# A two-stage Fourier kernel: its outer stages as float32 products on quarters of the array

## The chip, the cores and the metric

The kernel runs on one core of one Trainium2 chip. The metric is the time of one execution on the device in microseconds (us); of several executions the median is given. A profiled execution gives a trace: its span runs from the first to the last instruction.

## The reference

A Fourier layer with a soft threshold, followed by a layer that mixes by a two-dimensional Fourier transform and ends in an MLP:

```python
# x: (8, 3136, 256), float32
X = rfft(x, axis=1)
Yr = Xr @ w_r - Xi @ w_i + b_r;  Yi = Xr @ w_i + Xi @ w_r + b_i
Y = soft_threshold(Yr, 0.01) + 1j * soft_threshold(Yi, 0.01)
a = irfft(Y, n=3136, axis=1)
mixed = real(fft(fft(a, axis=1), axis=2))
u = a + mixed
un = (u - mean(u)) / sqrt(var(u) + 1e-6)          # over the last axis
out = u + relu(un @ w_ch1) @ w_ch2                # 256 -> 1024 -> 256
```

## The kernel before

The 3136 positions of a sequence are n1 (64) times n2 (49), and the transform along them is done in two stages of products with tables. Stage one, `p1`, multiplies 64 values of n1 by a 64 x 64 table and stores the result `a` in DRAM. Stage two, `p2_f2`, works along n2. Then come the weights (`p2_w`), the transform along the last axis for the mixing layer (`p2_mix`, which stores `md`), and the way back: `p2_yt` and `p2_g2` along n2, which store `b`, and `p3_norm` along n1. `p3_norm` loads `b` into `bf` and the mixed values into `mt`, multiplies `bf` by the inverse table, adds `mt` to get `ut`, and takes mean and variance; `p3_tr` transposes `ut` on TensorE, `p3_mlp1` and `p3_mlp2` are the MLP.

The 128 partitions hold two times 64 rows of n1: the two halves of a sequence's n2, 24 rows each, side by side. (The 25th row, `NM - 1`, is a single one that two neighbouring sequences share: the joint row.) So the tables `fwd` and `inv` are 128 x 128 with two blocks of 64 x 64 on the diagonal and zeros elsewhere. `p1` and `p3_norm` work in chunks of two n2 rows, 512 columns of 256 each.

Sequence 0 runs in float32 up to the inverse stage, and the forward stage of sequence 1 too (`te.matmul` with `fwd_f`). All else splits each operand into a high and a low part of type float32r and adds three products. ACT makes the high part, POOL (`lo_g`) or DVE (`lo_v`) the low part:

```python
def mm3(o, lh, ll, rh, rl, start=True, stop=True, first=0):
    ops = [(lh, rh), (lh, rl), (ll, rh)]
```

Each stage of each sequence is a generator that yields the time at which it would like to go on (in units of `T` per sequence); a heap hands them out in that order, and a scheduler orders each engine's instructions from there, taking one whose operands are late behind others. The engines then run their lists in order. The MLP works on groups of 4 n2 rows (`groups`; odd sequences have 25 rows, 4 groups of 4 and 3 of 3), and `clock3` gives each group its due time; `NRM` and `TR` say how long ahead of the MLP of a group its norm and its transposes stand. All DMAs go through SyncE's queue in order. `gtile` hands out 4 PSUM banks, shared by all stages but the MLP.

Of the kernel before, what the change touches and what calls it, by code (L numbers as in the profile page):

```python
# [10 lines left out]
F32 = mybir.dt.float32  # L11
# [38 lines left out]
def order_n2():  # L50

    return np.arange(NM * 2).reshape(2, NM).T.reshape(-1)[:N2]
# [8 lines left out]
def tables():  # L61
# [4 lines left out]
    inv = np.zeros((2, 2, U, 2, 32, 2))  # L66
    n1h = rows_n1()
    for s in range(2):
        for u in range(U):
            ph = 2 * np.pi * ((n1 * u) % N1) / N1  # L70
            if u == 0:
                alt = np.where(n1 % 2, -1.0, 1.0)
                fwd[s, :, s, 0, 0] = 1.0
                fwd[s, :, s, 1, 0] = alt
                inv[s, 0, 0, :, :, s] = 1.0
                inv[s, 1, 0, :, :, s] = np.where(n1h % 2, -1.0, 1.0)
            else:
                fwd[s, :, s, 0, u] = np.cos(ph)
                fwd[s, :, s, 1, u] = -np.sin(ph)
                phh = 2 * np.pi * ((n1h * u) % N1) / N1  # L80
                inv[s, 0, u, :, :, s] = 2 * np.cos(phh)
                inv[s, 1, u, :, :, s] = -2 * np.sin(phh)
# [54 lines left out]
def spectral_block(ctx: ExitStack, tc: tile.TileContext, x, w_ri, b_ri, w1, w2,  # L137
# [68 lines left out]
    fwd_f = cp.tile([128, 128], F32, name="fwd_f")  # L206
    fwd_0 = cp.tile([128, 128], F32, name="fwd_0")
# [11 lines left out]
    def load_consts():  # L219
# [14 lines left out]
        yield 1.6 * T  # L234
        for name in ("wr", "ws", "wd"):
            split(name, KF[name])
        split("fwd", fwd_f)

# [5 lines left out]
        inv = sb.tile([128, 128], F32, tag="mt", bufs=2, name="inv_f")  # L244
        nc.sync.dma_start(out=inv, in_=c_inv)
        split("inv", inv)
# [113 lines left out]
    def ask(b, ci, todo, slots, pre):  # L360

        tag, bufs, z, i = slots[ci]
        if i or ci in pre:
            return
        m, n = todo[ci]
        xf = pre[ci] = sb.tile([128, 512 * z], F32, tag=tag, bufs=bufs, name="xf")
        nn = n if n == 1 else 2 * z
        behind(BEHIND if b == 1 else 7, out=xf[:, :nn * D].rearrange("p (n d) -> p n d", d=D), in_=x_rows(b, m, nn))

    def p1(b):  # L370
# [8 lines left out]
        todo = chunks + [(NM - 1, 1)] * (b % 2 == 0)  # L379
        t0, width = T1 if b == 1 else (b - 0.3, 0.75)  # L380
        rooms = [("W2", 1, 4), ("W3", 1, 4)] + [("utl", 2, 2)] * 2 if b == 1 else [("xf", 2, 1)] * len(todo)
        slots = [(tag, bufs, z, i) for tag, bufs, z in rooms for i in range(z)]
        evs = [("bf", 2), ("bf", 2), ("bh", 2), ("bh", 2), ("bl", 2), ("bl", 2), ("ev", 2), ("ev", 2)] * 2
        pre = {}
        if b == 1:
            yield T * ASK
            for ci in range(0, 12, 2):
                ask(b, ci, todo, slots, pre)
        for ci, (m, n) in enumerate(todo):
            yield T * (t0 + width * ci / len(todo))  # L390
            w = n * D
            ask(b, ci, todo, slots, pre)
            tag, bufs, z, i = slots[ci]
            xf = pre[ci - i][:, i * 512:i * 512 + 512]
            g = gtile("g_f1")
            if b == 1:
                te.matmul(g[:, :w], fwd_f, xf[:, :w], start=True, stop=True)
            else:
                xh = sb.tile([128, 512], F32R, tag="xh", bufs=1, name="xh")
                xl = sb.tile([128, 512], F32R, tag="xl", bufs=1, name="xl")  # L400
                sc.copy(xh[:, :w], xf[:, :w])  # L401
                lo_g(xl[:, :w], xf[:, :w], xh[:, :w])
                mm3(g[:, :w], *K["fwd"], xh[:, :w], xl[:, :w])
            tag, bufs = evs[ci] if b == 1 else ("ev", 2)
            ev = sb.tile([128, 512], F32, tag=tag, bufs=bufs, name="ev")
            (va.tensor_copy if ci % 2 and b != 1 else sc.copy)(ev[:, :w], g[:, :w])
            evv = ev[:, :w].rearrange("p (n d) -> p n d", d=D)
            if n == 1:
                for r in range(2):
                    st_eng.dma_start(out=a_dram[b + r](0)[0][m, 0].rearrange("c u d -> (c u) d"), in_=evv[r * 64:r * 64 + 64, 0])  # L410
            else:
                st_eng.dma_start(out=n2_rows(a_dram[b](0)[0], m, n), in_=evv)
# [254 lines left out]
    def p2_g2(b):  # L667

        bd = b_dram[b] = dr.tile([NM, 2, 2, U, D], F32, tag="bd", bufs=4, name=f"bd{b}")
        for q in range(4):  # L670
            base, STEP, F2W, W0, WW, M0 = clock2(b, q)
            for i in range(4):
# [11 lines left out]
                bev = sb.tile([98, 512], F32, tag="bl" if b == 0 and i % 2 else "bev", bufs=2, name="bev")  # L684
# [6 lines left out]
    groups = [[(4 * i, 4) for i in range(6)], [(4 * i, 4) for i in range(4)] + [(16 + 3 * i, 3) for i in range(3)]]  # L691
    parts_of = {z: [(i, min(2, z - i)) for i in range(0, z, 2)] for z in (3, 4)}
# [6 lines left out]
    def p3_norm(b):  # L699

        for gi, (g0, z) in enumerate(groups[b % 2]):
            t0, T3 = clock3(b, g0)
            for i, n in parts_of[z]:
                yield t0 + T3 * (NRM + i / 4)
                yield from after(("b", b), ("m", b))
                m = g0 + i
                w = n * D
                joint = m == NM - 1

                bf = sb.tile([128, 512], F32, tag="bf", bufs=2, name="bf")  # L710
                mt = sb.tile([128, 2, D], F32, tag="mt", bufs=2, name="mt")
                bfv = bf[:, :w].rearrange("p (n d) -> p n d", d=D)
                if joint:
                    for r in range(2):
                        nc.sync.dma_start(out=bfv[64 * r:64 * r + 64, 0], in_=b_dram[b - 1 + r][m, 0].rearrange("c u d -> (c u) d"))
                else:
                    nc.sync.dma_start(out=bfv, in_=n2_rows(b_dram[b], m, n))
                for r in range(2):
                    bb, n2 = (b - 1 + r, m) if joint else (b, NM * r + m)
                    mpn, mmn = (d[0:NH].rearrange("(a n2) d -> a n2 d", n2=N2) for d in m_dram[bb])  # L720
                    if joint:
                        nc.sync.dma_start(out=mt[r:64:2, 0], in_=mpn[:, n2])
                    elif r == 0:
                        nc.sync.dma_start(out=mt[:64, :n], in_=bass.AP(
                            tensor=mpn.tensor, offset=mpn[:, n2].offset, ap=[[N2 * D, 32], [NM * D, 2], [1, n * D]]))
                    nc.sync.dma_start(out=mt[64 + r:128:2, :n][:, ::-1], in_=mmn[:, 49 - n2 - n:49 - n2])
                bh = sb.tile([128, 512], F32R, tag="bh", bufs=2, name="bh")
                bl = sb.tile([128, 512], F32R, tag="bl", bufs=2, name="bl")
                sc.copy(bh[:, :w], bf[:, :w])  # L729
# [4 lines left out]
                va.tensor_add(ut[:, :n], g[:, :w].rearrange("p (n d) -> p n d", d=D), mt[:, :n])  # L734
# [12 lines left out]
                gp.tensor_mul(vv[:, :n], vv[:, :n], rs[:, :n])
                gp.tensor_scalar(vv[:, :n], vv[:, :n], -0.5, 1.5, op0=ALU.mult, op1=ALU.add)
                gp.tensor_mul(rs[:, :n], rs[:, :n], vv[:, :n])
                uts[b, gi, i] = ut, rs  # L750

    def p3_tr(b):
        for gi, (g0, z) in enumerate(groups[b % 2]):
            t0, T3 = clock3(b, g0)
            for i, n in parts_of[z]:
# [5 lines left out]
                ut = uts[b, gi, i][0]  # L761
# [27 lines left out]
    def p3_mlp2(b):  # L789
        for gi, (g0, z) in enumerate(groups[b % 2]):  # L790
# [12 lines left out]
            for (i, n), o in zip(parts_of[z], ops):  # L803
                ut, rs = uts.pop((b, gi, i))
# [93 lines left out]
```

## Time and profile before

| | us |
|---|---|
| median of 3 runs | 1915.78 |
| lowest and highest | 1915.67, 1918.73 |
| profiled execution, its time | 1918.35 |
| profiled execution, its span | 1916.6 |
| TensorE busy (PE) | 1858.5 |
| VectorE, ScalarE, GpSimd busy | 1239.4, 838.5, 654.7 |

PE is TensorE's products, PEld its loads of weights, which run beside the products. A float32 product appears in the trace as two instructions of PE, each with a load of its own. A product's length in the trace contains its way through the array, so the lengths of neighbours overlap; the distance between two starts is what a product takes of the engine's time. The mean granted clock of TensorE was 0.984 of full speed. In the views, L162 is the line of `mm3`'s products; `g_f` is the bank of the forward stage, `g_g` that of the inverse stage (and of `p2_g2`), and `o` and `h` are those of the MLP.

### The profile page before, as it was taken

The numbers are of one execution on the slowest core, as the hardware profiler recorded it, in microseconds if no ns is written. First come the engines' busy times: TensorE is split into PE (matmuls) and PEld (weight loads), VectorE is DVE, ScalarE is ACT, GpSimd is POOL, SyncE is SP. The second block draws the span as 40 slices with busy tenths as digits, with TensorE's granted clock in tenths as the row PEclk, the third lists the DMA queues.
The fourth block names the chain that finished last, engine by engine and source line by source line (L and its number), as shares of the span: only waits on it lengthen the run. The fifth ranks groups of instructions, "written<-read, shape, count | busy, mean of one in ns | idle before, by whom it ended". The sixth has DMA issues, their size and how long they took to land.

```text
span 1916.6 us, 33595 instructions
## 1 busy us (share of the span) xinstructions
PE 1858.5 (97%) x12079; PEld 1698.1 (89%) x12079; DVE 1239.4 (65%) x2718; ACT 838.5 (44%) x1851; POOL 654.7 (34%) x1027
## 2 busy tenths in 40 slices
PE   6887999999999999999999999999999999999999
PEld 3557999999999999989999899998999999988999
DVE  3756767766666766667766666666677676665443
ACT  2455544444444444445444444434444343433222
POOL 0006543442334433244333344434334332322110
PEclk8998999999999999999999999999999999999999
DMA  8666543443435434354333543434443332223110
GB/s 247 217 195 197 156 125 101 138 136 111 135 97 154 133 104 120 99 159 138 110 112 105 151 130 114 118 105 135 139 123 101 106 100 65 76 80 109 59 37 25
DMA packets 153279, 232.93 MB, mean 122 GB/s; under 512 B 18256, under 2 KB 98200, under 8 KB 152856
## 3 DMA queue, kind: packets, MB, share of 16 engines
q1 hardware_dynamic: 153112, 230.78, 40.4%
q8 instruction: 95, 1.56, 0.3%
q14 instruction: 72, 0.59, 0.1%
HBM read 127.95 MB, written 102.76 MB: 120 GB/s over the span
## 4 chain that ended last, share of the span: by engine, by line
PE 86%; DMA 6%; DVE 2%; SPq 2%; ACT 2%; issue 1%; POOL 1%; DVEq 0%; POOLq 0%; ACTq 0%
PE o L162 27%; PE h L162 26%; PE g_w L162 9%; PE g_g L162 7%; PE g_f L465 4%; PE g_f L162 3%; PE g_yt L654 2%; PE g_ut L766 2%; PE g_mix L585 1%; DMA md<-mq 1%; DMA bf<-bd 1%; DMA raw_w<-in_w 1%; DMA mt<-md 1%; PE g_mix L587 1%; DMA af<-aq 1%
## 5 line engine op out<-in xcount | busy, mean ns | idle before, releaser
L786 DVE SCALAR_TENSOR_TENSOR hl<-h,hh 128x512 fp32r<-128x512 f32 (+1 forms) x416 | 272.8, 656 | 344.9 <-ACT hh L785 343.4
L162 PE MATMUL o<-w2h,hl 128*128 128x256 f32 x1568 | 454.6, 290 | 3.4 <-DVE hl L786 3.3
L785 ACT ACTIVATE hh<-h 128x512 fp32r<-128x512 f32 (+1 forms) x416 | 238.4, 573 | 491.3 <-PE h L162 448.3
L162 PE MATMUL o<-w2h,hh 128*128 128x256 f32 x1568 | 444.0, 283 | 0.0
L162 PE MATMUL o<-w2l,hh 128*128 128x256 f32 x1568 | 443.9, 283 | 0.0
L162 PE MATMUL h<-utl,w1h 128*128 128x512 f32 (+1 forms) x832 | 325.0, 391 | 0.0
L162 PE MATMUL h<-uth,w1l 128*128 128x512 f32 (+1 forms) x832 | 317.5, 382 | 0.0
L162 PE MATMUL h<-uth,w1h 128*128 128x512 f32 (+1 forms) x832 | 316.6, 381 | 0.0
L162 PEld LDWEIGHTS o<-w2h,hl 128*128 128x128 f32 x1568 | 298.7, 190 | 10.9 <-DVE hl L786 4.6
L162 PEld LDWEIGHTS o<-w2h,hh 128*128 128x128 f32 x1568 | 299.4, 191 | 6.1
L162 PEld LDWEIGHTS o<-w2l,hh 128*128 128x128 f32 x1568 | 299.3, 191 | 0.0
L155 POOL TENSOR_TENSOR bl<-bf,bh 128x512 fp32r<-128x512 f32 x104 | 128.2, 1234 | 278.6 <-ACT bh L729 268.7
L155 POOL TENSOR_TENSOR xl<-xf,xh 128x512 fp32r<-128x512 f32 (+1 forms) x75 | 100.5, 1340 | 277.7 <-ACT xh L401 277.4
L162 PEld LDWEIGHTS h<-uth,w1l 128*128 128x128 f32 x832 | 156.3, 188 | 24.9
L162 PEld LDWEIGHTS h<-utl,w1h 128*128 128x128 f32 x832 | 157.4, 189 | 15.2
L162 PEld LDWEIGHTS h<-uth,w1h 128*128 128x128 f32 x832 | 156.8, 188 | 14.5
L465 PEld LDWEIGHTS g_f<-tff,af 98*128 98x128 f32 x1024 | 146.8, 202 | 22.8 <-issue 11.3
L465 PE MATMUL g_f<-tff,af 98*128 98x100 f32 x1024 | 152.2, 282 | 11.3 <-DMA af<-aq 9.5
L734 DVE TENSOR_TENSOR ut<-g_g,mt 128x512 f32<-128x512 f32 x104 | 68.4, 657 | 82.4 <-PE g_g L162 55.5
L155 POOL TENSOR_TENSOR Xsl<-xs,Xsh 128x200 fp32r<-128x200 f32 x112 | 73.5, 657 | 134.9 <-ACT Xsh L491 129.5
L528 POOL TENSOR_TENSOR Y<-y,m 128x400 f32<-128x400 f32 x56 | 66.0, 1178 | 105.5 <-DVE m L527 78.0
L155 POOL TENSOR_TENSOR Xl<-xx,Xh 128x400 fp32r<-128x400 f32 x84 | 91.0, 1084 | 30.6 <-ACT Xh L482 30.6
(160 smaller groups left out, 3656.1 us busy)
## 6 DMA issues: line engine op xcount, KB each, us to landing
bd<-bev SPq DMA_DIRECT2D x128, 196.0 KB
bf<-bd SPq DMA_DIRECT2D x92, 256.0 KB
out_dram<-ut SPq DMA_DIRECT2D x92, 256.0 KB
af<-ad SPq DMA_DIRECT2D x56, 392.0 KB
md<-mq SPq DMA_DIRECT2D x112, 192.0 KB
ad<-ev SPq DMA_DIRECT2D x84, 256.0 KB
xf<-in_x SPq DMA_DIRECT2D x76, 256.0 KB
mt<-md SPq DMA_DIRECT2D x192, 64.0 KB
```

What stands on the lines that cost most here:

```text
L155: gp.tensor_sub(out_, full, hi.bitcast(F32))
L162: te.matmul(o, l, r, start=start and i == 0, stop=stop and i == 2)
L465: te.matmul(gf[:, k, :, s], afs[s][:, ui * D + k * 128:ui * D + k * 128 + 128], tfs[s][:, ui].rearrange("p (c j) -> p c j", c=2), start=Tr ...
L528: (va if b == 0 or o == 0 else gp).tensor_sub(y[:, o, :, c, :], y1, m)
L585: te.matmul(o, eh[:, e, ui], cs, start=e == 0, stop=False)
L587: te.matmul(o[:, :n], el[:, e, ui], cs[:, :n], start=False, stop=e == 1)
L654: te.transpose(gt[:100, (v * 2 + o) * 128:(v * 2 + o + 1) * 128], y[:, o, place].rearrange("p c j -> p (c j)"), ident)
L734: va.tensor_add(ut[:, :n], g[:, :w].rearrange("p (n d) -> p n d", d=D), mt[:, :n])
L766: te.transpose(gv[:, k, j * 128:(j + 1) * 128], ut[:, j, k * 128:(k + 1) * 128], ident)
L785: sc.activation(hh[:, :w], h[:, :w], AF.Relu)
L786: va.scalar_tensor_tensor(hl[:, :w], h[:, :w], 0.0, hh[:, :w].bitcast(F32), op0=ALU.max, op1=ALU.subtract)
```

## The change

The two outer stages no longer split their operands. A new helper, `quarters`, takes four n2 rows at a time and multiplies, in float32, each half of 64 partitions by its 64 x 64 block; the first two rows of a half write 64 partitions of a bank, the next two the other 64, and the two halves write two banks. The layouts follow: x is loaded 4 rows at a time in one transfer, `order_n2` and the rows of the tables of stage two are permuted, the inverse stage's rows come out with the half outside and n1 inside, `mt` is loaded for four rows by four transfers of 32 partitions, and `bf` by two ahead of the products. The joint rows are single float32 products on the whole array. In odd sequences the MLP's groups become five of 4, one of 2 and one of 3. Sequence 0's forward stage (`p1_first`) stays as it is.

```diff
+    def quarters(banks, mat, movs):
+        for j in range(2):
+            for i in range(2):
+                rows = slice(64 * i, 64 * i + 64)
+                te.matmul(banks[i][64 * j:64 * j + 64], mat[rows, rows], movs[i][j], start=True, stop=True)
...
     def p1(b):
-        todo = chunks + [(NM - 1, 1)] * (b % 2 == 0)
+        todo = [(m, 4) for m in range(0, NM - 1, 4)] + [(NM - 1, 1)] * (b % 2 == 0)
...
-            g = gtile("g_f1")
-            if b == 1:
-                te.matmul(g[:, :w], fwd_f, xf[:, :w], start=True, stop=True)
-            else:
-                xh = sb.tile([128, 512], F32R, tag="xh", bufs=1, name="xh")
-                xl = sb.tile([128, 512], F32R, tag="xl", bufs=1, name="xl")
-                sc.copy(xh[:, :w], xf[:, :w])
-                lo_g(xl[:, :w], xf[:, :w], xh[:, :w])
-                mm3(g[:, :w], *K["fwd"], xh[:, :w], xl[:, :w])
...
+            banks = [gtile("g_f1") for _ in range(2)]
+            quarters(banks, fwd_f, [[xf[64 * r:64 * r + 64, p * 512:p * 512 + 512] for p in range(2)] for r in range(2)])
+            for r, g in enumerate(banks):
+                tag, bufs = evs[(2 * ci + r) % len(evs)]
+                ev = sb.tile([128, 512], F32, tag=tag, bufs=bufs, name="ev")
+                (va.tensor_copy if r and b != 1 else sc.copy)(ev, g)
+                st_eng.dma_start(out=n2_rows(a_dram[b](0)[0], m + 2 * r, 2), in_=ev.rearrange("p (n d) -> p n d", d=D))
...
-    groups = [[(4 * i, 4) for i in range(6)], [(4 * i, 4) for i in range(4)] + [(16 + 3 * i, 3) for i in range(3)]]
+    groups = [[(4 * i, 4) for i in range(6)], [(4 * i, 4) for i in range(5)] + [(20, 2), (22, 3)]]
...
     def p3_norm(b):
-        for gi, (g0, z) in enumerate(groups[b % 2]):
-            t0, T3 = clock3(b, g0)
-            for i, n in parts_of[z]:
-                yield t0 + T3 * (NRM + i / 4)
...
-                sc.copy(bh[:, :w], bf[:, :w])
-                lo_g(bl[:, :w], bf[:, :w], bh[:, :w])
-                g = gtile("g_g1")
-                mm3(g[:, :w], *K["inv"], bh[:, :w], bl[:, :w])
-                ut = sb.tile([128, 2, D], F32, tag="ut", bufs=UTB, name="ut")
-                va.tensor_add(ut[:, :n], g[:, :w].rearrange("p (n d) -> p n d", d=D), mt[:, :n])
...
+        for m, n in [(4 * i, 4) for i in range(6)] + [(NM - 1, 1)] * (b % 2):
+            t0, T3 = clock3(b, m)
+            yield t0 + T3 * (NRM - 0.5 * (n == 1))
+            yield from after(("b", b), ("m", b))
+            mt = sb.tile([128, 4, D], F32, tag="mt", bufs=2, name="mt")
+            bfs = [sb.tile([128, 512], F32, tag="bf", bufs=4, name="bf") for _ in range(1 + (n > 1))]
+            for r in range(2):
+                if n == 1:
+                    nc.sync.dma_start(out=bfs[0][64 * r:64 * r + 64, :D], in_=b_dram[b - 1 + r][m, 0].rearrange("c u d -> (c u) d"))
                 else:
+                    nc.sync.dma_start(out=bfs[r].rearrange("p (n d) -> p n d", d=D), in_=n2_rows(b_dram[b], m + 2 * r, 2))
+            for r in range(2):
+                bb, n2 = (b - 1 + r, m) if n == 1 else (b, NM * r + m)
+                mpn, mmn = (d[0:NH].rearrange("(a n2) d -> a n2 d", n2=N2) for d in m_dram[bb])
+                p = 64 * r
+                nc.sync.dma_start(out=mt[p:p + 32, :n], in_=mpn[:, n2:n2 + n])
+                nc.sync.dma_start(out=mt[p + 32:p + 64, :n][:, ::-1], in_=mmn[:, 49 - n2 - n:49 - n2])
+            if n == 1:
                 g = gtile("g_g1")
+                te.matmul(g[:, :D], inv_f, bfs[0][:, :D], start=True, stop=True)
+                finish(m, 1, g, mt[:, :1])
+                continue
+            banks = [gtile("g_g1") for _ in range(2)]
+            quarters(banks, inv_f, [[bfs[r][64 * p:64 * p + 64] for r in range(2)] for p in range(2)])
+            for p, g in enumerate(banks):
+                finish(m + 2 * p, 2, g, mt[:, 2 * p:2 * p + 2])
```

`finish` holds what followed before: the sum into `ut`, the statistics, the square root and its correction, for two n2 rows.

More of the change, by code (lines that the diff above doesn't have):

```diff
@@ L50, in order_n2 @@
 def order_n2():
-    return np.arange(NM * 2).reshape(2, NM).T.reshape(-1)[:N2]
+    k = np.arange(NM - 1)
+    first = 4 * (k // 4) + k % 2 + NM * (k // 2 % 2)
+    return np.append(np.stack([first, first + 2], 1).reshape(-1), NM - 1)
 def rows_n1():
@@ L65, in tables @@
     fwd = np.zeros((2, N1, 2, 2, U))
-    inv = np.zeros((2, 2, U, 2, 32, 2))
+    inv = np.zeros((2, 2, U, 2, 2, 32))
     n1h = rows_n1()
@@ L74, in tables @@
                 fwd[s, :, s, 1, 0] = alt
-                inv[s, 0, 0, :, :, s] = 1.0
-                inv[s, 1, 0, :, :, s] = np.where(n1h % 2, -1.0, 1.0)
+                inv[s, 0, 0, s] = 1.0
+                inv[s, 1, 0, s] = np.where(n1h % 2, -1.0, 1.0)
             else:
@@ L80, in tables @@
                 phh = 2 * np.pi * ((n1h * u) % N1) / N1
-                inv[s, 0, u, :, :, s] = 2 * np.cos(phh)
-                inv[s, 1, u, :, :, s] = -2 * np.sin(phh)
+                inv[s, 0, u, s] = 2 * np.cos(phh)
+                inv[s, 1, u, s] = -2 * np.sin(phh)
     tf = np.zeros((2, N2, U, 2, S))
@@ L206, in spectral_block @@
     fwd_f = cp.tile([128, 128], F32, name="fwd_f")
+    inv_f = cp.tile([128, 128], F32, name="inv_f")
     fwd_0 = cp.tile([128, 128], F32, name="fwd_0")
@@ L234, in load_consts @@
         yield 1.6 * T
+        nc.sync.dma_start(out=inv_f, in_=c_inv)
         for name in ("wr", "ws", "wd"):
             split(name, KF[name])
-        split("fwd", fwd_f)
         cs = K["cs"] = cp.tile([128, 2, 2, 128], F32R, name="cs")
@@ L243, in load_consts @@
         sc.copy(cs[:, 0, 1, 0:1], t[:, 0, 128:129])
-        inv = sb.tile([128, 128], F32, tag="mt", bufs=2, name="inv_f")
-        nc.sync.dma_start(out=inv, in_=c_inv)
-        split("inv", inv)
     ident = cp.tile([128, 128], F32, name="ident")
@@ L365, in ask @@
         m, n = todo[ci]
-        xf = pre[ci] = sb.tile([128, 512 * z], F32, tag=tag, bufs=bufs, name="xf")
-        nn = n if n == 1 else 2 * z
+        xf = pre[ci] = sb.tile([128, 1024 * z], F32, tag=tag, bufs=bufs, name="xf")
+        nn = n if n == 1 else 4 * z
         behind(BEHIND if b == 1 else 7, out=xf[:, :nn * D].rearrange("p (n d) -> p n d", d=D), in_=x_rows(b, m, nn))
+    def quarters(banks, mat, movs):
[3 more added lines that the diff above has]
+                te.matmul(banks[i][64 * j:64 * j + 64], mat[rows, rows], movs[i][j], start=True, stop=True)
     def p1(b):
@@ L378, in p1 @@
                 a_dram[i] = lambda u, ad=ad: (ad, u)
-        todo = chunks + [(NM - 1, 1)] * (b % 2 == 0)
+        todo = [(m, 4) for m in range(0, NM - 1, 4)] + [(NM - 1, 1)] * (b % 2 == 0)
         t0, width = T1 if b == 1 else (b - 0.3, 0.75)
-        rooms = [("W2", 1, 4), ("W3", 1, 4)] + [("utl", 2, 2)] * 2 if b == 1 else [("xf", 2, 1)] * len(todo)
+        rooms = [("W2", 1, 2), ("W3", 1, 2)] + [("utl", 2, 1)] * 2 if b == 1 else [("xf", 2, 1)] * len(todo)
         slots = [(tag, bufs, z, i) for tag, bufs, z in rooms for i in range(z)]
-        evs = [("bf", 2), ("bf", 2), ("bh", 2), ("bh", 2), ("bl", 2), ("bl", 2), ("ev", 2), ("ev", 2)] * 2
+        evs = [("bf", 4)] * 4 + [("ev", 2)] * 2 if b == 1 else [("ev", 2)]
         pre = {}
@@ L386, in p1 @@
             yield T * ASK
-            for ci in range(0, 12, 2):
+            for ci in range(len(todo)):
                 ask(b, ci, todo, slots, pre)
@@ L390, in p1 @@
             yield T * (t0 + width * ci / len(todo))
-            w = n * D
             ask(b, ci, todo, slots, pre)
-            tag, bufs, z, i = slots[ci]
-            xf = pre[ci - i][:, i * 512:i * 512 + 512]
-            g = gtile("g_f1")
-            if b == 1:
-                te.matmul(g[:, :w], fwd_f, xf[:, :w], start=True, stop=True)
-            else:
-                xh = sb.tile([128, 512], F32R, tag="xh", bufs=1, name="xh")
-                xl = sb.tile([128, 512], F32R, tag="xl", bufs=1, name="xl")
-                sc.copy(xh[:, :w], xf[:, :w])
-                lo_g(xl[:, :w], xf[:, :w], xh[:, :w])
-                mm3(g[:, :w], *K["fwd"], xh[:, :w], xl[:, :w])
[L404 to L407, printed above, removed]
+            i = slots[ci][3]
+            xf = pre[ci - i][:, i * 1024:i * 1024 + 1024]
             if n == 1:
+                g = gtile("g_f1")
+                te.matmul(g[:, :D], fwd_f, xf[:, :D], start=True, stop=True)
+                ev = sb.tile([128, 512], F32, tag="ev", bufs=2, name="ev")
+                sc.copy(ev[:, :D], g[:, :D])
                 for r in range(2):
-                    st_eng.dma_start(out=a_dram[b + r](0)[0][m, 0].rearrange("c u d -> (c u) d"), in_=evv[r * 64:r * 64 + 64, 0])
-            else:
-                st_eng.dma_start(out=n2_rows(a_dram[b](0)[0], m, n), in_=evv)
+                    st_eng.dma_start(out=a_dram[b + r](0)[0][m, 0].rearrange("c u d -> (c u) d"), in_=ev[r * 64:r * 64 + 64, :D])
+                continue
[6 more added lines that the diff above has]
+                st_eng.dma_start(out=n2_rows(a_dram[b](0)[0], m + 2 * r, 2), in_=ev.rearrange("p (n d) -> p n d", d=D))
         done.add(("a", b))
@@ L683, in p2_g2 @@
                         mm3(g[:98, cols], tih[:, t], til[:, t], yh[:, cols], yl[:, cols], first=1)
-                bev = sb.tile([98, 512], F32, tag="bl" if b == 0 and i % 2 else "bev", bufs=2, name="bev")
+                bev = sb.tile([98, 512], F32, tag="xf" if b == 0 and i % 2 else "bev", bufs=2, name="bev")
                 (va.tensor_copy if b else sc.copy)(bev, g[:98])
@@ L688, in p2_g2 @@
         done.add(("b", b))
-    groups = [[(4 * i, 4) for i in range(6)], [(4 * i, 4) for i in range(4)] + [(16 + 3 * i, 3) for i in range(3)]]
-    parts_of = {z: [(i, min(2, z - i)) for i in range(0, z, 2)] for z in (3, 4)}
+    groups = [[(4 * i, 4) for i in range(6)], [(4 * i, 4) for i in range(5)] + [(20, 2), (22, 3)]]
+    parts_of = {z: [(i, min(2, z - i)) for i in range(0, z, 2)] for z in (2, 3, 4)}
     uts, uthl, hhl = {}, {}, {}
@@ new lines, in finish @@
+        def finish(m, n, g, mt):
+            ut = sb.tile([128, 2, D], F32, tag="ut", bufs=UTB, name="ut")
+            va.tensor_add(ut[:, :n], g[:, :n * D].rearrange("p (n d) -> p n d", d=D), mt)
+            st = sb.tile([128, 2, 6], F32, tag="st", bufs=2, name="st")
+            ag = sb.tile([128, 2, 2], F32, tag="ag", bufs=2, name="ag")
+            rs = sb.tile([128, 2, 1], F32, tag="rs", bufs=8, name="rs")
+            for j in range(n):
+                va.bn_stats(st[:, j], ut[:, j])
+                va.bn_aggr(ag[:, j], st[:, j])
+            vv = sb.tile([128, 2, 1], F32, tag="vv", bufs=2, name="vv")
+            sc.activation(rs[:, :n], ag[:, :n, 1:2], AF.Sqrt, bias=eps_t)
+            gp.tensor_scalar(vv[:, :n], ag[:, :n, 1:2], 1.0, EPS, op0=ALU.mult, op1=ALU.add)
+            va.reciprocal(rs[:, :n], rs[:, :n])
+            gp.tensor_mul(vv[:, :n], vv[:, :n], rs[:, :n])
+            gp.tensor_mul(vv[:, :n], vv[:, :n], rs[:, :n])
+            gp.tensor_scalar(vv[:, :n], vv[:, :n], -0.5, 1.5, op0=ALU.mult, op1=ALU.add)
+            gp.tensor_mul(rs[:, :n], rs[:, :n], vv[:, :n])
+            uts[b, m] = ut, rs
@@ L890 @@
         for r in range(2):
-            v = y[:, h, :, r]
+            v = y[:, r, h]
             for s in range(2):
```

45 lines of the change are left out of this document (5 added, 40 removed).

## The prediction

> **What bounds the kernel now.** I read the page's parts 1, 2 and 4 first: who is busy, at which clock, and which engine carries the chain.
>
> ```profile
> PE 1858.5 (97%) x12079; PEld 1698.1 (89%) x12079; DVE 1239.4 (65%) x2718; ACT 838.5 (44%) x1851; POOL 654.7 (34%) x1027
> ...
> PEclk8998999999999999999999999999999999999999
> ...
> PE 86%; DMA 6%; DVE 2%; SPq 2%; ACT 2%; issue 1%; POOL 1%; DVEq 0%; POOLq 0%; ACTq 0%
> ```
>
> TensorE is busy for 97% of the span, at the full granted clock in almost every slice, and carries 86% of the chain that ended last. No other engine is over 65%. So the time of this kernel is the time that TensorE needs for its list of products, plus the few places where it stands still. The waits of PE, longest first, say how few these are:
>
> ```profile
> PE g_ut L766 <- DVE ut L734: 17.1, 5, 5.7
> PE g_f L465 <- DMA af<-aq: 9.5, 1, 9.5
> PE g_f L338 <- DMA xf<-in_x: 4.4, 3, 3.7
> PE g_g L162 <- ACT bh L729: 3.9, 1, 3.9
> ```
>
> Only the first belongs to the changed stages: the transposes of `p3_tr` wait five times for the sum `ut` of `p3_norm`. Work taken from ACT, DVE or POOL is therefore worth nothing by itself; work taken from TensorE counts almost one to one.
>
> **The terms removed.** The groups by line with shapes kept apart give the counts. `g_g<-bh` is the last inverse stage, `g_f<-xh` and `g_f<-xf,fwd_f` the first forward one.
>
> ```profile
> L162 PE MATMUL g_g<-bh,invh 128*128 128x512 f32 x92 | 39.8, 432 | 3.9 <-ACT bh L729 3.9
> L162 PE MATMUL g_f<-xh,fwdh 128*128 128x512 f32 x72 | 31.5, 438 | 2.4 <-ACT xx L481 1.8 <-ACT xh L401 0.6
> L397 PE MATMUL g_f<-xf,fwd_f 128*128 128x512 f32 x24 | 12.3, 595 | 0.0
> L162 PE MATMUL g_g<-bh,invh 128*128 128x256 f32 x12 | 3.9, 322 | 0.0
> L162 PE MATMUL g_f<-xh,fwdh 128*128 128x256 f32 x3 | 0.9, 284 | 0.0
> ```
>
> Each of the first two stands for three products of a chunk (`mm3`). The mean of one there includes its pipeline and must not be added up: what a product costs TensorE is the distance to the next start, read from the timeline of PE.
>
> ```profile
> 562.31 0.33 PE L162 MATMUL h<-utl,w1h 128*128 128x384 f32 x1
> 562.48 0.33 PE L162 MATMUL h<-uth,w1h 128*128 128x384 f32 x1
> ...
> 566.49 0.40 PE L162 MATMUL g_g<-bl,invh 128*128 128x512 f32 x1
> 566.72 0.39 PE L162 MATMUL g_g<-bh,invl 128*128 128x512 f32 x1
> 566.95 0.27 PE L162 MATMUL o<-w2h,hl 128*128 128x256 f32 x1
> ...
> 586.45 0.28 PE L162 MATMUL g_g<-bh,invh 128*128 128x256 f32 x1
> 586.57 0.29 PE L162 MATMUL g_g<-bl,invh 128*128 128x256 f32 x1
> ...
> 90.01 1.02 PE L397 MATMUL g_f<-xf,fwd_f 128*128 128x512 f32 x2
> 90.87 0.50 PE L511 MATMUL g_w<-X,wsf 128*128 128x400 f32 x1
> ```
>
> A float32r product of 512 columns takes 0.23 us, of 384 columns 0.17, of 256 columns 0.12; one float32 product of 512 columns is two instructions and takes 0.86 us, so 0.43 an instruction. The stages cost now, without waits: 92 + 72 = 164 chunks x 3 x 0.23 = 113.2 us; 15 single-row chunks x 3 x 0.12 = 5.4; the 12 chunks of sequence 1 (24 instructions) x 0.86 = 10.3. Together 128.9 us.
>
> **The terms added.** `quarters` is called 6 times for each of 7 sequences forward and 8 inverse: 90 calls, each for two former chunks. Of the 15 single-row chunks 7 are left (3 forward, 4 inverse; the other 8 were odd rows of groups of 3, and go into the calls); each becomes one float32 product of 256 columns: 7 x 0.43 = 3.0 us. One call is four float32 products of 64 x 64 and 512 columns, so eight instructions of 0.43 us each if a quarter streams a column as fast as the whole array does. No row shows a product on a quarter. The bounds: all eight in a row, 8 x 0.43 = 3.44 us; the four quarters side by side, 2 x 0.43 = 0.86. On top come the loads of the weights and, perhaps, an array that must empty when its form changes:
>
> ```profile
> 83.96 1.00 PEld L465 LDWEIGHTS g_f<-tff,af 98*128 98x128 f32 x8 [0.53 <-ACT X L474]
> ...
> L397 PE MATMUL g_f<-xf,fwd_f x24: 591/592/618, 83.2 to 129.5; 128*128 128x512 f32 x24
> ```
>
> Eight float32 loads of 128 columns end in 1.00 us, at most 0.125 each, so I estimate 0.06 for 64 columns; emptying costs what a product lasts beyond its distance to the next, 0.592 - 0.43 = 0.16 us. Side by side, the price is 0.86 at least, and 0.86 + 7 x 0.06 (the last quarter's first product behind seven loads) + 2 x 0.16 (emptied before and after) = 1.60 at most. PEld is busy 89% of the span beside a PE at 97%, that is, loads hide behind other products here, so I take one load and one emptying: 0.86 + 0.06 + 0.16 = 1.08 us. 90 x 1.08 + 3.0 = 100.2 us, a saving of 128.9 - 100.2 = 28.7 us.
>
> On this price the Trainium skill, in TensorEngine Tiling (Array Packing), Key Properties, says that a change of the tiling mode drains TensorE while a change of tile does not. No row here has a second mode; by that rule both emptyings are paid, a call costs 1.24 us and the sum would save 14 us instead of 29.
>
> **What moves beside it.** The casts and the subtractions for the split go, and their tiles:
>
> ```profile
> L729 ACT CAST bh<-bf 128x512 fp32r<-128x512 f32 x104 | 61.9, 595 | 45.5 <-PE g_g L162 25.0 <-DMA bf<-bd 19.1
> L401 ACT CAST xh<-xf 128x512 fp32r<-128x512 f32 (+1 forms) x75 | 46.1, 615 | 20.9 <-PE g_f L162 16.2 <-DMA xf<-in_x 3.5 <-DMA mt<-md 0.7
> ...
> L155 POOL TENSOR_TENSOR bl<-bf,bh 128x512 fp32r<-128x512 f32 x104 | 128.2, 1234 | 278.6 <-ACT bh L729 268.7 <-PE g_g L162 6.2 <-DMA bf<-bd 3.3
> L155 POOL TENSOR_TENSOR xl<-xf,xh 128x512 fp32r<-128x512 f32 (+1 forms) x75 | 100.5, 1340 | 277.7 <-ACT xh L401 277.4
> ```
>
> ACT loses 108 us and POOL 229, both off the path: nothing. Banks, evacuations (`ev`, the sum into `ut`) and statistics keep their count: nothing; a call takes two of the four `g` banks at once, as two chunks did one after the other. The groups of the odd sequences' MLP go from 4,4,4,4,3,3,3 to five of 4, one of 2, one of 3: the 3 x 48 = 144 products of 384 columns (24.5 us) become 48 each of 512, 256 and 384 (48 x 0.52 = 25.0), +0.5 us for each of four sequences, +2. Out stores and the `b` and `a` stores keep their bytes. The splits of `fwd` and `inv`, two operations on ACT and two on DVE, go once, and `inv_f` loads once as before: nothing.
>
> The transfers merge: one load of x for two, and for `mt` four loads of 32 rows for two former parts with three loads each, so SP issues less. But all of a call's loads now stand ahead of its first sum, and this matters where a sequence starts, since `p3_norm` waits there for the last store of `md`. This is the place of the 17.1 us above. The chain that ended last, in order of time, around 600 us (start, length, what):
>
> ```profile
> 595.49 3.69 DMA md<-mq
> ...
> 599.19 0.58 SPq L724
> ...
> 599.82 0.61 SPq L726
> ...
> 600.47 2.30 DMA mt<-md
> ```
>
> The timeline of PE at the starts of sequences 2 and 3, and the stretches behind both (busy time of each engine, granted clock, DMA share, GB/s):
>
> ```profile
> 603.73 1.09 PE L766 MATMUL g_ut<-ident,ut 128*128 128x128 f32 x4 [3.48 <-DVE ut L734]
> ...
> 829.38 0.38 PE L162 MATMUL o<-w2h,hl 128*128 128x256 f32 x1 [0.53 <-DVE hl L786]
> ```
>
> ```profile
> 600.00:604.00 4.00, 0.53 (x4) 0.30 (x3) 1.11 (x3) 0.49 (x1) 1.73 (x3) 0.84 0.72 219
> 604.00:611.00 7.00, 7.00 (x37) 7.00 (x36) 2.14 (x8) 0.70 (x2) 0.97 (x5) 0.60 0.63 187
> 830.00:837.00 7.00, 5.86 (x36) 5.01 (x35) 2.89 (x6) 2.66 (x6) 2.52 (x3) 1.00 0.67 204
> ```
>
> The transposes wait 3.48 us for the sum, the sum for `mt`, `mt` for `md`. With the change one more issue (0.6 us) stands in that chain, and 0.25 MB more has to land, 1.2 us at the 219 GB/s of that stretch: +0.6 to +1.8 us. Queued behind on PE is everything, as the transposes are next in its order. What is saved, the cast and the subtraction, was done while `md` was awaited, so nothing. I take +1.0 for each of 7 starts, +7 us; at the least 0. After the wait of 3.48 us the granted clock is 0.60 over 7 us, which costs 2.8 us more; after one of 0.53 us at 829 it stays at 1.00.
>
> **The sum.** -28.7 + 2 + 7 = -19.7 us. The profiled execution took 1918.35 us around its span of 1916.6; the median of the runs is 1915.78, and the sum is put on that: 1896 us, about 1.0% faster.
>
> **The rivals.**
> Strict order: products start one after the other as they stand in the program, and a quarter's second piece has to follow its first. Then each new quarter's first piece starts only beside the second piece of the one before: five rounds, 5 x 0.43 = 2.15 us a call. For it speaks that one float32 product is two instructions, next to each other, on the same cells; against it nothing in this trace, as nothing runs on a part of the array. 90 x 2.15 + 3 - 128.9 + 9 = +67.6: 1983 us, slower. It decides from a call of (128.9 - 3 - 9) / 90 = 1.30 us on.
> Beside this stands the Trainium skill, TensorE: Matmul & The Clock Gate, Part 3 on packing small matmuls: it states that products of different tiles overlap with starts some 4 ns apart, but also that they stay in program order in start and end, and its measured cases do not say what two pieces on one tile do. The second statement is this rival; the trace cannot choose.
> Two at a time: only quarters of different rows (or columns) run together. Four rounds, 1.72 us: 90 x 1.72 + 3 - 128.9 + 9 = +37.9: 1954 us; where the second pair starts beside the first one's second piece it is three rounds, 1.29 us, and no change.
> Starts: the quarters run side by side, but the longer wait trips the low clock at the four sequence starts that keep it now. Each loses 3.5 + 2.8 us, the other three 1 to 2: 4 x 6.3 + 3 x 1.5 = 30 us in place of the 7. Total -28.7 + 2 + 30 = +3: 1919 us. For it: the 3.48 us row; against it: the rows at 829, where no such wait stands and the clock holds.
>
> **How the numbers follow.** The likeliest case, side by side, gets 0.56; its own range goes from 0.86 a call with free starts (1869) to 0.86 + 0.06 + 2 x 0.16 = 1.24 a call with starts at 1.8 (1916). Strict order 0.18, two at a time 0.14, starts 0.12. The range runs from 1862, a little below the first case's bound, for waits that shrink with less work on ACT and POOL, to 1955, which takes in two at a time; outside it lies strict order, with 0.18, and little else. Within 0.2% (3.8 us) is what a measurement of this kernel cannot tell from no change. Faster: 0.53 from side by side, 0.03 each from three rounds and from starts, 0.59; same: 0.03 + 0.05 + 0.02 = 0.10; slower: 0.18 + 0.09 + 0.04 = 0.31.
>
> **What the profile after would show.** Right: `quarters` with 8 instructions a call whose starts lie in pairs or fours closer than 0.1 us, about 1.1 us from a call's first start to the next other product; PE's products fewer in time, ACT down 108 us and POOL down 229. Wrong by order: starts of one call 0.43 us apart, PE still at 97% and longer. Wrong by starts: a longer wait of `g_ut` for `ut`, in seven places, with a granted clock near 0.6 in the 7 us behind it at starts that keep 1.00 now. Also wrong would be a new wait of PE for `g` banks, or for `bf` to land ahead of the quarters.

## The result, and the profile after

| | us | runs |
|---|---|---|
| before, median (lowest to highest) | 1917.26 (1915.67 to 1918.82) | 4 |
| changed, median (lowest to highest) | 1944.91 (1941.39 to 1951.58) | 4 |
| ratio, 95% interval | 1.0148 (1.0119 to 1.0178) | |

The change made the kernel 1.5% slower, by about 28 us. 1896 was forecast, faster, with a range up to 1955: the measured time lies inside the range and on the wrong side of no change. The profiled execution is the slowest of the four: 1951.58 us around a span of 1949.4.

From the page of the changed kernel, the same three rows as shown of before:

```profile
PE 1887.6 (97%) x12252; PEld 1619.3 (83%) x12252; DVE 1200.5 (62%) x2704; ACT 744.4 (38%) x1662; POOL 413.2 (21%) x828
...
PEclk8896999999999999999999999999999999999999
...
PE 86%; DMA 5%; DVE 4%; SPq 2%; issue 1%; ACT 1%; POOL 1%; DVEq 0%; ACTq 0%; POOLq 0%
```

ACT lost 94 us and POOL 241, about as forecast. But PE got 29 us more of busy time where it should have lost some 27; its share of the span is 97% as before. Two digits of the clock differ: the second slice fell from 9 to 8, and the fourth, 146 to 195 us, from 8 to 6. The groups of PE with shapes kept apart, the new products (8 instructions a call, 90 calls):

```profile
L374 PE MATMUL g_g<-bf,inv_f 64*64 64x512 f32 x384 | 79.4, 634 | 7.4 <-DMA bf<-bd 7.4
L374 PE MATMUL g_f<-xf,fwd_f 64*64 64x512 f32 x336 | 64.1, 639 | 8.4 <-DMA xf<-in_x 8.4
```

Here the busy time counts overlapped instructions once: 143.5 us for 90 calls is 1.59 a call, while a call in one piece is busy for 1.09. The timeline of PE shows both. First a whole call with its neighbours (start, length, ..., count of merged instructions):

```profile
689.39 0.40 PE L164 MATMUL h<-uth,w1l 128*128 128x512 f32 x1
689.72 1.09 PE L374 MATMUL g_f<-xf,fwd_f 64*64 64x512 f32 x8
690.74 0.36 PE L164 MATMUL g_g<-yl,tih 100*98 100x256 f32 x1
690.93 0.28 PE L164 MATMUL g_g<-yh,tih 100*98 100x256 f32 x1
```

Then a call of which only half of the instructions stand at a place; the halves are 5.46 us apart:

```profile
996.29 1.08 PE L374 MATMUL g_g<-bf,inv_f 64*64 64x512 f32 x4
...
1001.42 0.40 PE L164 MATMUL h<-uth,w1l 128*128 128x512 f32 x1
1001.75 1.07 PE L374 MATMUL g_g<-bf,inv_f 64*64 64x512 f32 x4
1002.75 0.45 PE L164 MATMUL g_w<-Xh,wdh 128*128 128x400 f32 x1
1003.04 0.34 PE L164 MATMUL g_w<-Xl,wdh 128*128 128x400 f32 x1
```

Eight instructions take 1.02 us to the next other product, four take 1.00. Around both, the neighbours lose some more: the `h` ahead of either is 0.33 us from its successor instead of 0.23, the `g_w` behind the half 0.29 instead of 0.18. Over all calls of the trace the medians are 0.09 us of entry, 1.02 and 0.10 of exit, 1.22 us, for a whole call, and 0.09, 1.01 and 0.10, 1.20 us, for a half. **A half costs as much as a whole**, and by the order of PE's instructions only 57 of the 90 calls stand whole; 33 are broken, 24 of them between the two banks, 9 in other ways (most into six and two instructions, two calls into three pieces). That is 35 pieces more than 90. (The expectations below speak of 34 broken calls; by 1.2 us apiece it is nearly the same sum.) Where pieces of two calls meet they stand at one place: in the trace, the quarters' products stand at 122 places with other products between them.

The longest waits of PE in the changed kernel:

```profile
PE g_f L467 <- DMA af<-aq: 8.5, 1, 8.5
PE g_f L374 <- DMA xf<-in_x: 8.4, 1, 8.4
PE g_ut L764 <- DVE ut L706: 7.7, 4, 2.8
PE g_g L374 <- DMA bf<-bd: 7.4, 2, 6.0
```

The transposes' wait for `ut`, 17.1 us before, is down to 7.7. New are the waits of `quarters` itself: for `xf`, once, and for `bf`. The first of these stands at the first call of sequence 2; the timelines of PE and of SP there:

```profile
136.77 0.61 PE L584 MATMUL g_mix<-csf,ef 128*100 128x129 f32 x4
145.81 1.98 PE L374 MATMUL g_f<-xf,fwd_f 64*64 64x512 f32 x8 [8.44 <-DMA xf<-in_x]
```

```profile
137.11 1.43 SPq L689 DMA_DIRECT2D bd<-bev  x2
138.59 1.39 SPq L278 DMA_DIRECT2D xf<-in_x  x1
```

The load of x is issued right behind two stores of `bev`. In the changed kernel `p2_g2` gives every other `bev` of sequence 0 one of the two `xf` buffers (before, it was one of `bl`, which the change drops; the diff shown above leaves this line out), so the load must wait until that store has read it. The stretch from 140 to 190 us, changed kernel and then before (PE, PEld, DVE, ACT, POOL busy, granted clock, DMA share, GB/s):

```profile
140.00:190.00 50.00, 31.48 (x130) 20.17 (x131) 16.14 (x40) 12.99 (x29) 9.09 (x19) 0.62 0.75 208
```

```profile
140.00:190.00 50.00, 38.44 (x219) 34.01 (x217) 29.61 (x63) 29.49 (x65) 30.87 (x43) 0.83 0.68 205
```

130 instructions of PE in place of 219, at a clock of 0.62 in place of 0.83. By the starts of the first `o` product of the MLP the changed kernel is 15.0 us behind (193.95 against 178.91), and at the last one 32.9 (1945.15 against 1912.27): the start and a slow loss after it, about 2.6 us a sequence, are two separate things.

### The profile page after: what moved, and what is told of

It is laid out like the page before. It is cut to its first block, busy times and chain, and to the rows that moved or that the text cites. A ratio compares the mean times of both kernels' runs of the same rounds, so it can differ in the third digit from the quotient of the medians.

```text
span 1949.4 us, 33124 instructions
## 1 busy us (share of the span) xinstructions
PE 1887.6 (97%) x12252; PEld 1619.3 (83%) x12252; DVE 1200.5 (62%) x2704; ACT 744.4 (38%) x1662; POOL 413.2 (21%) x828
## 3 DMA queue, kind: packets, MB, share of 16 engines
q8 instruction: 97, 1.59, 0.3%
## 4 chain that ended last, share of the span: by engine, by line
PE 86%; DMA 5%; DVE 4%; SPq 2%; issue 1%; ACT 1%; POOL 1%; DVEq 0%; ACTq 0%; POOLq 0%
PE o L164 27%; PE h L164 26%; PE g_w L164 9%; PE g_f L467 5%; PE g_g L164 4%; PE g_g L374 3%; PE g_yt L656 2%; PE g_f L374 2%; PE g_ut L764 2%; PE g_mix L587 1%; DMA md<-mq 1%; PE g_w L513 1%; DMA mt<-md 1%; DMA raw_w<-in_w 1%; DMA xf<-in_x 1%
## 5 line engine op out<-in xcount | busy, mean ns | idle before, releaser
L784 DVE SCALAR_TENSOR_TENSOR hl<-h,hh 128x512 fp32r<-128x512 f32 (+2 forms) x416 | 273.1, 657 | 409.3 <-ACT hh L783 407.7
L164 PE MATMUL o<-w2h,hl 128*128 128x256 f32 x1568 | 460.1, 293 | 4.0 <-DVE hl L784 3.4
L783 ACT ACTIVATE hh<-h 128x512 fp32r<-128x512 f32 (+2 forms) x416 | 238.2, 572 | 566.1 <-PE h L164 512.7
L164 PE MATMUL h<-utl,w1h 128*128 128x512 f32 (+2 forms) x832 | 325.5, 391 | 0.0
L164 PE MATMUL h<-uth,w1l 128*128 128x512 f32 (+2 forms) x832 | 317.9, 382 | 0.0
L164 PE MATMUL h<-uth,w1h 128*128 128x512 f32 (+2 forms) x832 | 317.7, 382 | 0.0
L467 PEld LDWEIGHTS g_f<-tff,af 98*128 98x128 f32 x1024 | 141.7, 202 | 37.4 <-issue 18.4
L715 POOL TENSOR_SCALAR vv<-ag 128x2 f32<-128x2 f32 (+1 forms) x100 | 21.9, 219 | 602.5 <-DVE ag L712 574.6
L527 DVE SCALAR_TENSOR_TENSOR y<-g_w,bias,ks 128x400 f32<-128x400 f32 x128 | 80.4, 629 | 58.5 <-PE g_w L164 40.3
L706 DVE TENSOR_TENSOR ut<-g_g,mt 128x512 f32<-128x512 f32 (+1 forms) x100 | 65.4, 673 | 67.9 <-DMA mt<-md 41.4
```

What stands on the lines that cost most here:

```text
L164: te.matmul(o, l, r, start=start and i == 0, stop=stop and i == 2)
L467: te.matmul(gf[:, k, :, s], afs[s][:, ui * D + k * 128:ui * D + k * 128 + 128], tfs[s][:, ui].rearrange("p (c j) -> p c j", c=2), start=Tr ...
L527: va.scalar_tensor_tensor(y1, gw, bias[:, c, o:o + 1], ks, op0=ALU.add, op1=ALU.add)
L706: va.tensor_add(ut[:, :n], g[:, :n * D].rearrange("p (n d) -> p n d", d=D), mt)
L783: sc.activation(hh[:, :w], h[:, :w], AF.Relu)
L784: va.scalar_tensor_tensor(hl[:, :w], h[:, :w], 0.0, hh[:, :w].bitcast(F32), op0=ALU.max, op1=ALU.subtract)
```

## The experiments

My theory: calls broken by the order of PE's list (some 35 further pieces at 1.2 us), plus some 14 us of start from the shared `xf` buffers; the price of a whole call is 1.22 us and is no loss. The rivals: the form of the products itself costs too much; or the float32 data path (four rows awaited at once, no split chain) is what delays.

**Calls kept whole.** A one-element copy into the second bank waits for that bank and for the call's last load; the first product waits for the copy, the other three follow directly.

```diff
+        hold = va.tensor_copy(banks[1][64:65, :1], movs[1][1][:1, :1])
...
+                    first = te.matmul(...); tc.add_manual_dep(first.ins, hold.ins.name, ...)
+                    with tc.high_priority(), tc.issue_after(first.ins): te.matmul(...)
```

> Each call of the four quarters is kept whole in TensorE's order (a copy of one element into the second bank makes the first product wait for both banks and both loads; the other three follow at once). Theory 'broken calls': a call that the scheduler broke in two costs 1.2 us for each half, as much as a whole one; 34 of 90 calls are broken, so 34 x 1.2 = 41 us less than the changed kernel: about 1904 us, faster than before. Rival 'waits': the calls lose by waiting for banks and loads, which are now waited for in one place; no gain, 1940 to 1955 us.

Measured: 1918.75 us (1917.18 to 1923.48, 10 runs), ratio to before 1.0009 (0.9994 to 1.0024), 26 us less than the changed kernel. All 90 calls are whole. The timeline of PE shows two of them back to back, at half clock (0.50 from 159 to 163 us; L377 is the first quarter, here one piece of it, three of L382 are the same piece of the others):

```profile
159.03 1.08 PE L377 MATMUL g_g<-bf,inv_f 64*64 64x512 f32 x1 [6.45 <-DVE g_f L371]
159.04 1.12 PE L382 MATMUL g_g<-bf,inv_f 64*64 64x512 f32 x3
159.91 1.06 PE L377 MATMUL g_g<-bf,inv_f 64*64 64x512 f32 x1
...
160.76 1.06 PE L377 MATMUL g_f<-xf,fwd_f 64*64 64x512 f32 x1
...
161.62 1.06 PE L377 MATMUL g_f<-xf,fwd_f 64*64 64x512 f32 x1
```

These are not four calls 0.86 us apart but two, one inverse and one forward, each with two rounds; at half clock a round takes 0.86 us, and the second call begins as if it were the first one's third round. So the mechanism holds, and the time shows its size only in part: 41 us were expected. PE's busy time did fall by 41.8 us (1887.6 to 1845.8), but PE stands idle for some 10 us more: calls now wait where broken ones had gone on with a half. The waits of PE name the copy:

```profile
PE g_f L377 <- DVE g_f L371: 13.3, 5, 8.3
PE g_f L475 <- DVE ut L714: 11.3, 3, 7.9
...
PE g_g L377 <- DVE g_f L371: 6.4, 1, 6.4
```

8.3 of the 13.3 us are the late `xf` at the start, which this kernel still has; the 6.4 us stand where the changed kernel waits 6.0 us for `bf`.

**The start alone.** `bev` takes a buffer of `ut`, which sequence 0 doesn't need yet, not of `xf`.

```diff
-  bev = sb.tile([98, 512], F32, tag="xf" if b == 0 and i % 2 else "bev", bufs=2, ...)
+  bev = sb.tile([98, 512], F32, tag="ut" if b == 0 and i % 2 else "bev", bufs=UTB if b == 0 and i % 2 else 2, ...)
```

> Sequence 0's odd bev tiles take buffers of ut instead of those of xf; TensorE's order is the same, product by product. Theory 'start': the 8.4 us wait of the first call of sequence 2 for its x is that buffer, taken by bev until its store is done; 8 to 13 us less, about 1934 us. Rival: the wait is TensorE's order or the queue; within 3 us of 1945.

Measured: 1930.7 us (1927.81 to 1939.52, 6 runs), ratio 1.0072 (1.0045 to 1.0099): 14 us less than the changed kernel, with PE's order of instructions unchanged. The stretch from 140 to 190 us:

```profile
140.00:190.00 50.00, 37.56 (x211) 29.07 (x212) 28.11 (x66) 20.57 (x48) 18.05 (x37) 0.76 0.66 194
```

211 instructions instead of 130, clock 0.76. The first `o` product comes 0.1 us ahead of before, the last one 9.9 behind: the start is repaired, a slow loss stays.

**All calls broken.** Each bank's pair gets a turn of its own, half a chunk later, with its own `gtile`.

```diff
-            quarters(banks, fwd_f, ...)
+            for r in range(2):
+                if r: yield T * (t0 + width * (ci + 0.5) / len(todo))
+                g = gtile("g_f1"); half(g, fwd_f, r, ...)
```

> Every call is issued as two halves, one row group (and bank) each, half a chunk's time apart, so that nearly all are apart in TensorE's order (150 of 168 pieces are halves, some quarters). Theory 'broken calls': about 56 more calls broken at 1.2 us each, 67 us more than the changed kernel, about 2010 us. Rival 'waits' (a half holds one bank only and waits for less): no slower than the changed kernel, 1925 to 1945 us.

Measured: 2013.18 us (2006.92 to 2019.45, 2 runs), ratio 1.049 (1.0434 to 1.0547), 68 us over the changed kernel. No call is whole now, some are in three or four pieces, and the quarters' products stand at 186 places instead of 122: 64 more, 1.06 us each. The groups of the same 720 instructions:

```profile
L373 PE MATMUL g_g<-bf,inv_f 64*64 64x512 f32 x384 | 114.8, 629 | 0.0
L373 PE MATMUL g_f<-xf,fwd_f 64*64 64x512 f32 x336 | 101.1, 642 | 10.8 <-DMA xf<-in_x 10.8
```

The mean of one is as before (629 and 642 ns), and the busy time is 215.9 us in place of 143.5: the same instructions, overlapped less.

**Both repairs.** The calls kept whole and `bev` apart.

> Both edits: whole calls and bev apart from xf. If both theories hold and do not cover each other: 1945 - 41 - 10 = about 1894 us, 1.2% faster than before. If only the start holds: 1934. If only whole calls count: 1904.

Measured: 1909.28 us (1903.9 to 1910.84, 6 runs), ratio 0.9949 (0.9927 to 0.997). With the start repaired, whole calls are worth 21 us (1930.7 to 1909.28). The expected 1894 again took the full 1.2 us for each broken call. Where the rest goes can be read from the pages: PE's busy time, and what is left of the profiled span beside it.

| | places | PE busy, us | rest of the span, us |
|---|---|---|---|
| changed | 122 | 1887.6 | 61.8 |
| all calls broken | 186 | 1965.6 | 52.1 |
| calls kept whole | 87 | 1845.8 | 72.1 |
| the start alone | 122 | 1877.5 | 49.0 |
| both repairs | 87 | 1841.0 | 61.1 |

The busy time follows the places: 64 more cost 78.0 us (1.22 each), 35 fewer save 41.8 (1.19) and, with the start repaired, 36.5 (1.04). The idle time moves against it: breaking all calls takes 10 us of it away, keeping them whole adds 10 and 12. So a whole call saves PE's time as the theory says, and gives part of it back by waiting for both banks and all its loads.

**The list and the chain apart.** The kernel before, with its layouts, but one float32 product on the whole array per chunk instead of three float32r ones, and so without the splits.

```diff
-                sc.copy(xh[:, :w], xf[:, :w]); lo_g(xl[:, :w], xf[:, :w], xh[:, :w])
-                mm3(g[:, :w], *K["fwd"], xh[:, :w], xl[:, :w])
+                te.matmul(g[:, :w], fwd_f, xf[:, :w], start=True, stop=True)   # likewise inv_f, bf
```

> The kernel before, with one float32 product of the whole 128 x 128 table for each chunk in place of the split and the three float32r products: no quarters, old layouts. Theory 'TensorE's list': a chunk costs 0.86 instead of 0.70 us, 152 chunks beyond sequence 1's 12, and 15 single rows 0.43 instead of 0.36: 164 x 0.17 = 28 us more than before, about 1945 us, whatever ACT and POOL lose. Rival 'the split costs too': with 229 us less on POOL and 108 less on ACT, waits go and the time stays within 10 us of before.

Measured: 1924.26 us (1921.52 to 1927.55, 6 runs), ratio 1.0044 (1.0032 to 1.0056). The list of products alone is 164 x (0.86 - 0.69) = 28 us longer, and 1 for the single rows (15 x 0.07); the time rose by 8. So the rival was right: the split chain that goes gives back about 20. The two profiles say in what form: PE is busy for 22 us longer, not 29 (1880.4 against 1858.5), and idle for 39 us of the span instead of 58. The windows show one place: behind the start of sequence 2 in this kernel, in before, and in the changed one (whose start stands later):

```profile
592.00:612.00 20.00, 17.95 (x132) 16.88 (x131) 9.60 (x28) 8.79 (x22) 5.81 (x15) 1.00 0.62 182
```

```profile
592.00:612.00 20.00, 16.52 (x106) 16.05 (x105) 9.34 (x23) 8.48 (x22) 9.57 (x19) 0.83 0.65 189
```

```profile
620.00:640.00 20.00, 18.30 (x128) 16.22 (x125) 11.20 (x32) 8.17 (x22) 4.15 (x13) 0.91 0.84 248
```

132 and 128 instructions of PE against 106, at a clock of 1.00 and 0.91 against 0.83. The waits of `g_ut`, 17.1 us before, are down in this kernel too:

```profile
PE g_ut L752 <- DVE ut L720: 8.7, 4, 2.7
```

Which of the removed operations on ACT and POOL had held `ut` back was not separated.

**The price of the form.** The kernel with both repairs, each call's products computed twice (the second time over the first), so that 16 instructions stand in a call.

```diff
-        for j in range(2):
+        for j in range(4):        # row and bank of j % 2
```

> Whole calls and bev apart, and each call's four products issued twice in a row (the second time over the same banks, same values). Theory 'change of form': a call is two rounds of 0.43 us and 0.36 us for emptying the array at both ends, which a second set of rounds does not pay again: 90 x 0.86 = 77 us more than that kernel (1909), about 1986 us. Rival 'price of a call': 1.22 us each time, 110 us more, 2019 us.

Measured: 1989.28 us (1987.59 to 1990.97, 2 runs), ratio 1.0382 (1.0361 to 1.0402), 80 us over the kernel with both repairs, 0.89 a call: two more rounds of 0.43 and next to nothing else. From the timeline of PE:

```profile
706.21 0.64 PE L377 MATMUL g_f<-xf,fwd_f 64*64 64x512 f32 x1
706.22 0.65 PE L382 MATMUL g_f<-xf,fwd_f 64*64 64x512 f32 x3
706.69 0.59 PE L377 MATMUL g_f<-xf,fwd_f 64*64 64x512 f32 x1
706.70 1.46 PE L382 MATMUL g_f<-xf,fwd_f 64*64 64x512 f32 x11
708.09 0.36 PE L164 MATMUL g_g<-yl,tih 100*98 100x256 f32 x1
```

These rows also settle the order: the first piece of the first quarter starts at 706.21, those of the other three within 0.02 us of it, and only at 706.69 the first quarter's second piece. The doubled call takes 1.88 us to the next other product, a plain one 1.02. So of 1.22 us two rounds are 0.86, and 0.36 is paid once for each change of form, however much stands in between.

**The copy on another engine.** Both repairs, with the one-element copy on ACT, which is 40% busy, in place of DVE.

```diff
-        hold = va.tensor_copy(banks[1][64:65, :1], movs[1][1][:1, :1])
+        hold = sc.copy(banks[1][64:65, :1], movs[1][1][:1, :1])
```

> Whole calls and bev apart, the one-element copy that holds a call until its banks and loads are there on ACT (38% busy) instead of DVE (62%). Theory: DVE runs its list in order, so a hold that waits keeps back the sums and the high and low parts behind it; on ACT it keeps back less: 2 to 6 us under 1909, 1903 to 1907 us. Rival: ACT's relu and casts stand behind it just so; 1909 or more.

Measured: 1903.5 us (1901.57 to 1906.36, 4 runs), ratio 0.9932 (0.9916 to 0.9949), the fastest version here, 0.7% ahead of before and 41 us ahead of the changed kernel. From its page and its waits of PE:

```profile
PE 1841.5 (97%) x12252; PEld 1611.7 (85%) x12252; DVE 1198.7 (63%) x2704; ACT 754.3 (40%) x1752; POOL 408.8 (21%) x828
```

```profile
PE g_f L475 <- DVE ut L714: 11.9, 3, 6.9
PE g_g L377 <- ACT g_g L371: 9.8, 1, 9.8
...
PE g_ut L772 <- DVE ut L714: 6.0, 4, 3.2
```

PE is busy 46 us less than in the changed kernel with the same 12252 instructions: an engine at 97% was not at its floor. By the medians this is 5.8 us better than with the copy on DVE, but the intervals overlap, and the two profiled executions (1905.28 here, 1903.9 there) don't show it. Two whole calls back to back at full clock, from its timeline of PE:

```profile
670.95 0.64 PE L377 MATMUL g_g<-bf,inv_f 64*64 64x512 f32 x1
...
671.43 0.59 PE L377 MATMUL g_g<-bf,inv_f 64*64 64x512 f32 x1
...
671.86 0.59 PE L377 MATMUL g_f<-xf,fwd_f 64*64 64x512 f32 x1
...
672.29 0.59 PE L377 MATMUL g_f<-xf,fwd_f 64*64 64x512 f32 x1
...
672.83 0.39 PE L164 MATMUL o<-w2h,hl 128*128 128x256 f32 x1
```

The rounds are 0.48, 0.43, 0.43 and 0.54 us apart: the first and the last pay for the change of form, the call's border in the middle nothing.

**Fewer banks.** If the wait for a second bank makes the scheduler break calls, three `g` banks instead of four must break more. The changed kernel, and as a control the kernel before, with the same edit:

```diff
-  (gtile)  bufs=4
+  (gtile)  bufs=3
```

> The changed kernel with 3 instead of 4 banks for gtile. In TensorE's order 65 calls are then broken in two between the banks, 24 were. Theory 'a missing second bank breaks the calls': 31 more broken calls in all at 1.2 us, 37 us more than the changed kernel, 1982 us, and a few us beside for what three banks cost the other stages. Rival: calls break by late loads; within 15 us of 1945.

> The kernel before with 3 instead of 4 banks for gtile: the measure for what three banks cost without quarters. Theory: its pieces may stand apart at no price, so it loses little, under 8 us (1916 to 1924), and the 40 us between the changed kernel with 3 and with 4 banks are broken calls. Rival: 3 banks cost any kernel 25 us or more, and the 40 us say nothing on calls.

Measured: the changed kernel 1985.18 us (1983.53 to 1986.84, 2 runs), ratio 1.036 (1.0339 to 1.0381), with 66 calls broken instead of 33, 65 of them between the two banks, where 24 were; the kernel before 1924.41 (1921.98 to 1930.73, 8 runs), ratio 1.0031 (1.0012 to 1.005). Of the 40 us more, 7 are the control's; the other 33 over 30 more places (152 instead of 122) are 1.1 us each. One bank fewer breaks calls, and what it costs is nearly all the price of broken calls; the bank itself is worth little.

## Why the prediction was wrong

**The step that failed** is "Banks, evacuations ... keep their count: nothing; a call takes two of the four `g` banks at once, as two chunks did one after the other", and with it the count "90 calls" of eight instructions in one piece. The scheduler is told nothing of a call. Where a call's second bank comes free later than its first, it puts other products in between, as the kernels with three banks show (for the nine calls broken otherwise, a late `bf` is the likely cause; it was not tried). The trace then shows no wait for a bank, one of the two that the prediction had named as signs; it shows four instructions where eight should stand, and each of the 35 further pieces takes 1.2 us. The three kernels that change the number of places and little else agree on its weight: 64 more cost 68 us, 30 more 33 us, 35 fewer gained 21 (with the start repaired), or 36.5 of PE's busy time less 12 of further waits, since a whole call must wait for both banks and all its loads. Whether the place of the copy shortens these waits is not shown.

The other sign that was named, a wait for `bf`, did come: 7.4 us, at the first inverse call of the kernel (158 us). Before, PE waited there too, 3.9 us for `bh` and 5.7 for `ut`. With the start repaired the wait for `bf` is still 8.1 us, yet the MLP begins no later than before, so this sign stands for no loss of its own.

**The price of a call** was mis-sized: 1.08 us taken, 1.22 measured, 90 x 0.14 = 12.6 us. Of the two emptyings I hid one behind other work, since weight loads hide there; it is paid at both ends (0.09 and 0.10 us lost by the neighbours, 0.16 within the call). The rule of the Trainium skill that stood beside this step, TensorEngine Tiling (Array Packing), Key Properties, that a change of the tiling mode drains TensorE, gave 1.24; the trace, with 1.22, agrees with it. The saving of the products, had every call been whole, is then 128.9 - 90 x 1.22 - 3.0 = 16 us.

**The rivals of order** fell. The quarters run four wide. (The sum of strict order was also wrong: 90 x 2.15 + 3 - 128.9 + 9 is 76.6, not 67.6, so 1992 us and not 1983.) The Trainium skill, TensorE: Matmul & The Clock Gate, Part 3 on packing small matmuls, states starts some 4 ns apart. From start to start the trace has 6 to 7 ns. The strict order that the rival took from one product to the next does not hold for the two pieces here: the other quarters' first pieces start ahead of the first quarter's second piece, 0.46 us earlier. In the kernel a product is one instruction; in which order TensorE is handed its two pieces, the trace does not show.

**The starts** came out with the wrong sign. I added 7 us for longer waits, and a rival 30; the waits of `g_ut` fell by 9.4 us. And "ACT loses 108 us and POOL 229, both off the path: nothing" was wrong: float32 on the whole array, without the split, got 20 us back, as less idle time of PE. The prediction's own list of waits had a sign of it. It says that only the first line belongs to the changed stages, but the fourth, 3.9 us of `g_g` for `bh`, is the inverse stage waiting for the cast that goes. How the rest of the 20 us comes about stays open. A real start cost did appear, but near the kernel's own start and not at every sequence's, 14 us from a shared buffer in `p2_g2`, which the prediction did not look at.

**The account.** -16 (products at the true price) + 42 (35 further pieces) + 14 (start) - 9 (waits of `ut`) + 2 (the MLP's groups, not measured by itself) = +33; the medians differ by 28, the two profiled executions by 33. That it fits so closely is in part chance, as the terms are not additive: taking away the 42 gained 21 to 27, and the split chain alone was worth 20, not 9. It is luck, too, that the measured 1945 lies inside the range: the range reached up to 1955 for "two at a time", which the traces rule out.

## What to carry to other kernels

When an edit pays only if several instructions run next to each other, ask what keeps them next to each other in the engine's list: with a scheduler between program and engine, one late buffer is enough to split them, and nothing in the waits tells of it. Count the pieces in the timeline before trusting a price per call, and let the first instruction wait for everything that the group needs. Before putting a buffer to a second use, look at whose load stands behind it.

## What the runs showed of the hardware that was not expected

- Four float32 products of 64 x 64 on the array's quarters start 6 to 7 ns apart and take together what one whole-array product takes, 0.86 us for both pieces. Two on two quarters take nearly as long: 1.00 us to the next other product, against 1.02 for four.
- Going from whole-array products to quarters and back costs 0.36 us on top, the same for two rounds as for four: 1.02 us from first start to the next other product for 8 instructions, 1.88 for 16, and in both cases some 0.1 us lost by the neighbour on either side.
- Calls that follow each other directly pay that price once between them: 1.88 us for two.
